# A gated linear attention over 128-token chunks by levels, rewritten over 64-token chunks with logarithms, angles and one masked score product

## The chip, the cores and the metric

The kernel runs on one core of one Trainium2 chip. A core has a matrix engine (PE, with its weight loads shown apart as PEld), a vector engine (DVE), an activation engine (ACT), a general engine (POOL), and SyncE (SP), whose queue issues most of the transfers. Each engine runs its own list of instructions in order; semaphores tie the lists together. The metric is device time in microseconds, less being better.

## The reference

Two blocks follow one another. The first is a recurrence with a complex decay for each feature, the second an MLP with ELU between its two products.

```python
B, H, S, D = (4, 8, 768, 48)
mag = np.sqrt(a_re * a_re + a_im * a_im)
scale = np.minimum(mag, 0.999) / (mag + 1e-06)
a_re_n, a_im_n = (a_re * scale, a_im * scale)
for t in range(S):
    ar, ai = (a_re_n[:, :, t, :, None], a_im_n[:, :, t, :, None])
    new_re = ar * S_re - ai * S_im
    new_im = ar * S_im + ai * S_re
    kv = np.einsum('bhd,bhe->bhde', k[:, :, t], v[:, :, t])
    S_re, S_im = (new_re + kv, new_im)
    y[:, :, t] = np.einsum('bhd,bhde->bhe', q[:, :, t], S_re)
# x = y as (B*S, H*D) = (3072, 384)
h = x @ w_in                       # (384, 2048)
g = np.where(h > 0.0, h, np.exp(np.minimum(h, 0.0)) - 1.0)
return g @ w_out                   # (2048, 384)
```

q, k and v are normal numbers times 0.1. a_re lies between 0.85 and 0.95, a_im is normal with a spread of 0.1. The two MLP weights arrive as float64 and are made float32 on the chip.

## The kernel before

A group is 256 tokens of one batch, two chunks of 128; there are twelve. Heads stand two by two on the partitions, tokens along the free dimension. Within a chunk, a query and a key meet at one of seven levels (blocks of 2, 4, .. 128 tokens). At each level `totals` (before the levels) multiplies decays over blocks, `scores` (the matmuls of L277) multiplies keys with queries, and `widen` carries both to blocks of twice the length by complex products: of queries on DVE, of keys on POOL (both in `product`, L247 to L251), with ACT copying the other half (L332). After every second level `values` masks the scores on DVE (L288) and multiplies them with values (L304). No logarithm and no division by a decay occurs. `normalise` makes the decays with a square root (L190) and a reciprocal (L192). `finish` adds what earlier chunks give (L343), transposes keys (L354) and makes the next state (L360). `begin` transposes inputs (L206).

`seam` moves y by ten transfers (L384) so that heads stand one after another. `hidden` (L397 and the activations L403 to L406) and `project` (L414, L419) are the MLP. They are called one level at a time in the next group's loop, so that they fall between its scores. `load_weights` (L154 to L176) takes one tile of float64 words through four DVE operations, an addition on POOL (L172) and a last DVE operation; four such tiles are called after each level of the first group until all 28 (12 of w_in, 16 of w_out) are done. The order of instructions on each engine is made by the tile framework's scheduler from the written order.

## Time and profile before

| | |
|---|---|
| median of 3 runs | 1701.83 us (1701.32 to 1703.79) |
| span of the profiled execution | 1704.6 us |
| the profiled execution's own time | not given apart from its span, which is 0.16% above the median |
| PE busy / weight loads | 1193.1 us (70%) / 922.5 us (54%) |
| DVE busy | 1289.6 us (76%) |
| POOL busy | 893.2 us (52%) |
| ACT busy | 439.2 us (26%) |
| bytes over the DMA queues | 69.67 MB, mean 41 GB/s |
| mean granted PE clock | 0.819 |

Busy time is the union of an engine's instructions. A matmul of float32 appears as two records in the profile, a transpose as one. A row of the timeline gives start, length, engine, line, operation, output and inputs, shapes, count, and in brackets the idle time before it with what ended it. A row of the groups gives the count, the busy time, the mean length in ns, and the idle time before with its releasers. A row of the waits gives the total, the number and the longest. A row of windows gives the stretch, busy time and count of PE, PEld, DVE, ACT and POOL, and then the granted clock, DMA share and rate.

### The profile page before, as it was taken

How to read it: one execution, taken by the hardware profiler on the slowest of the kernel's cores; microseconds unless marked ns; L12 is line 12 of the kernel's file. 1: busy time of each engine (PE TensorE's matmuls, PEld its weight loads, DVE VectorE, ACT ScalarE, POOL GpSimd, SP SyncE). 2: the span in 40 equal slices, each digit the busy share in tenths (PEclk: the TensorE clock that was granted, in tenths of full speed). 3: DMA queues.
4: the chain of work that ended last, by engine and by line, in shares of the span. 5: the costliest groups of instructions: out<-in, count | busy, mean ns of one | idle time of the engine just before them, and what ended most of it. 6: DMA issues, size and time to landing. Idle time of an engine off the chain costs nothing.

```text
span 1704.6 us, 26958 instructions
## 1 busy us (share of the span) xinstructions
PE 1193.1 (70%) x10464; PEld 922.5 (54%) x10464; DVE 1289.6 (76%) x1860; ACT 439.2 (26%) x865; POOL 893.2 (52%) x835
## 2 busy tenths in 40 slices
PE   3522368948848847866876874894893893894989
PEld 2521355637637636655654653663662763773766
DVE  7897888788788777867868868858858858858831
ACT  2010043124124123122322331331421521311313
POOL 6574464665465464544654654645545645635610
PEclk8555679778978978987996996996895996996999
DMA  5413330030031040022022013013012012010000
GB/s 108 107 54 108 116 60 11 18 72 17 18 67 26 18 76 16 15 59 37 12 51 49 12 47 51 8 38 65 8 38 54 20 34 45 13 33 23 2 19 10
DMA packets 156895, 69.67 MB, mean 41 GB/s; under 512 B 134496, under 2 KB 142432, under 8 KB 156768
## 3 DMA queue, kind: packets, MB, share of 16 engines
q1 hardware_dynamic: 156768, 67.94, 17.8%
q8 instruction: 84, 1.38, 0.4%
q14 instruction: 43, 0.35, 0.1%
HBM read 36.44 MB, written 4.72 MB: 24 GB/s over the span
## 4 chain that ended last, share of the span: by engine, by line
PE 45%; DVE 44%; issue 4%; POOL 3%; ACT 2%; DMA 1%; SPq 1%; POOLq 0%; DVEq 0%
PE bank L414 15%; PE a L277 11%; DVE pq L248 8%; DVE pq L247 8%; PE bank L397 8%; PE y L304 6%; DVE T L250 4%; DVE T L251 4%; DVE Q L251 3%; DVE Q L250 3%; DVE r L192 3%; DVE a_sb L288 2%; DVE g L406 2%; POOL wp L172 2%; DVE Q L224 2%
## 5 line engine op out<-in xcount | busy, mean ns | idle before, releaser
L277 PE MATMUL a<-Q,K 48*64 48x128 f32 (+1 forms) x4992 | 350.6, 291 | 334.7 <-DVE Q L250 291.3
L277 PEld LDWEIGHTS a<-Q,K 48*64 48x64 f32 x4992 | 307.1, 149 | 387.5 <-issue 275.9
L250 POOL TENSOR_TENSOR K<-pk,pk 128x256 f32<-128x256 f32 x168 | 145.0, 863 | 408.0 <-PE a L277 400.4
L397 PE MATMUL bank<-x,w_in 128*128 128x256 f32 x1152 | 305.3, 421 | 13.2 <-ACT er L404 8.9
L332 ACT COPY K<-K 128x256 f32<-128x256 f32 x336 | 137.5, 445 | 566.6 <-PE a L277 492.1
L397 PEld LDWEIGHTS bank<-x,w_in 128*128 128x128 f32 x1152 | 232.9, 209 | 66.1 <-issue 22.8
L414 PE MATMUL bank<-w_out,g 128*128 128x384 f32 x768 | 267.0, 501 | 0.1
L247 POOL TENSOR_TENSOR pk<-K,T 128x512 f32<-128x512 f32 x168 | 208.6, 1242 | 67.8 <-DVE T L250 50.4
L248 POOL TENSOR_TENSOR pk<-K,T 128x512 f32<-128x512 f32 x168 | 231.0, 1375 | 0.0
L250 DVE TENSOR_TENSOR Q<-pq,pq 128x256 f32<-128x256 f32 x168 | 109.5, 652 | 131.7 <-PE a L277 126.0
L414 PEld LDWEIGHTS bank<-w_out,g 128*128 128x128 f32 x768 | 143.7, 193 | 98.9 <-issue 11.2
L304 PE MATMUL y<-a_sb,vl 128*64 128x128 f32 (+1 forms) x1344 | 119.5, 316 | 98.3 <-DVE a_sb L288 98.3
L248 DVE TENSOR_TENSOR pq<-Q,T 128x512 f32<-128x512 f32 x168 | 174.7, 1040 | 0.0
L247 DVE TENSOR_TENSOR pq<-Q,T 128x512 f32<-128x512 f32 x168 | 166.6, 992 | 3.9
L304 PEld LDWEIGHTS y<-a_sb,vl 128*64 128x64 f32 (+1 forms) x1344 | 94.3, 163 | 134.3 <-DVE a_sb L288 115.5
L406 DVE SCALAR_TENSOR_TENSOR g<-ee,er 128x512 f32<-128x512 f32 x96 | 85.5, 893 | 89.8 <-ACT ee L405 89.8
L251 POOL TENSOR_TENSOR K<-pk,pk 128x256 f32<-128x256 f32 x168 | 149.0, 887 | 0.0
L251 DVE TENSOR_TENSOR Q<-pq,pq 128x256 f32<-128x256 f32 x168 | 131.8, 785 | 0.0
L288 DVE TENSOR_TENSOR a_sb<-a,masks 128x1024 f32<-128x1024 f32 x72 | 87.4, 1214 | 55.7 <-PE a L277 55.7
L403 ACT ACTIVATE ee<-bank 128x512 f32<-128x512 f32 x96 | 57.1, 595 | 234.0 <-PE bank L397 179.6
L247 DVE TENSOR_TENSOR pq<-T 128x512 f32<-128x512 f32 (+6 forms) x168 | 100.5, 598 | 17.5 <-ACT T L219 12.4
L248 DVE TENSOR_TENSOR pq<-T 128x512 f32<-128x512 f32 (+6 forms) x168 | 97.3, 579 | 0.0
(68 smaller groups left out, 1261.2 us busy)
## 6 DMA issues: line engine op xcount, KB each, us to landing
w<-in_moe_w_in_dram SPq DMA_DIRECT2D x12, 512.0 KB
vl<-vn SPq DMA_DIRECT2D x48, 128.0 KB
vl<-vn SPq DMA_DIRECT2D x96, 64.0 KB
vl<-vn SPq DMA_DIRECT2D x192, 32.0 KB
w<-in_moe_w_out_dram SPq DMA_DIRECT2D x16, 384.0 KB
ar<-in_a_re_dram SPq DMA_DIRECT2D x24, 192.0 KB
ai<-in_a_im_dram SPq DMA_DIRECT2D x24, 192.0 KB
kn<-in_k_dram SPq DMA_DIRECT2D x24, 192.0 KB
```

The lines of the kernel that those rows point to most:

```text
L247: eng.tensor_tensor(out=t1, in0=x, in1=y_re, op=ALU.mult)
L248: eng.tensor_tensor(out=t2, in0=x, in1=y_im, op=ALU.mult)
L250: eng.tensor_tensor(out=to_re, in0=seen(t1[:, 0]), in1=seen(t2[:, 1]), op=minus)
L251: eng.tensor_tensor(out=to_im, in0=seen(t1[:, 1]), in1=seen(t2[:, 0]), op=plus)
L277: nc.tensor.matmul(x["a"][ts(row, HP), z, ts(p, n)], lhsT=x["K"][rows, i, ts(p, C // 2)], rhs=x["Q"][rows, i, ds((p + 1) * C - n, n)], sta ...
L288: nc.vector.tensor_tensor(out=a, in0=x["a"].rearrange("p j (x t) -> p j x t", t=C), in1=masks[:, n].unsqueeze(1).unsqueeze(1).to_broadcast ...
L304: nc.tensor.matmul(to, **got, start=False, stop=False, skip_group_check=True)
L332: nc.scalar.copy(out=to[:, i, 1], in_=seen(old[:, i, 1]))
L397: nc.tensor.matmul(t[:, e], lhsT=w_in[:, i, ts(f0 + f + e, C)], rhs=x[:, i], start=(i == 0), stop=(i == NI - 1),)
L403: nc.scalar.activation(out=e, in_=t, func=AF.Relu, scale=-1.0)
L406: nc.vector.scalar_tensor_tensor(out=g[:, f : f + 2], in0=e, scalar=-1.0, in1=r, op0=ALU.add, op1=ALU.add)
L414: nc.tensor.matmul(t, lhsT=gs[f // FB][:, f % FB, ts(c, C)], rhs=w_out[:, f], start=(f == 0), stop=(f == NF - 1),)
```

## The change

The kernel is now split in two. The old one without its weights becomes `_general`, and stands behind a branch at the end (L906). Ahead of it stands a new one that does the whole computation. It takes units of 128 tokens of two batches (again 256 tokens, twelve units). `squares` and `logarithms` make, for each element, half the logarithm of the squared magnitude, capped, and the tangent's argument of the angle; `angles` takes the arctangent; `turns` and `decays` sum angles over the tokens and logarithms over 64 tokens by a matmul with a triangle of ones (L628, L650); `waves` takes sine and cosine, and `gated` multiplies keys by the inverse decay and queries by the decay, with sine and cosine beside each other (96 numbers a head). Then one score product for each 64 tokens (L712), masked once on DVE, replaces the seven levels; `states` (L733) and `values` (L757, L766) follow, and `hidden` (L801) and `project` (L817) as before, where ELU is now max(exp(min(h,0)) - 1, h), with one Relu less.

While it computes, it records for each unit the least a_re and the greatest |a_im|. `verdict` compares both with 0.7, and every engine reads the result and branches: where any element falls outside, the old kernel runs too and overwrites the output.

The order is written out by hand, in 15 steps of 16 slots: at step s the first stage (A) works on unit s, B on s - 1, C on s - 2, and the MLP (M) on s - 3. The weights are converted one a slot from step 0.

```diff
@@ -14,25 +14,31 @@
-C = 128  # tokens of a chunk, the length over which decays are multiplied out
+C = 128
+L = 64
...
+LEAST_RE = 0.7
+MAGIC = 1.5 * 2.0**23
+TURN = 6.2831850
...
-def tile_gateloop__then__act_elu_kernel(
+def _general(
...
+@with_exitstack
+def tile_gateloop__then__act_elu_kernel(
...
+    NB = 2
+    NU = B // NB * (S // C)
+    GT = NB * C
...
+    def work(shape):
+        return ps.tile(shape, FP32, tag="w", bufs=3, name="w")
...
+    def squares(u):
+        x = nat[u]
+        ar, ai = x["ar"], x["ai"]
+        nc.vector.tensor_reduce(
+            out=least[:, u : u + 1], in_=flat(ar), axis=mybir.AxisListType.X, op=ALU.min
+        )
+        nc.vector.tensor_reduce(
+            out=most[:, u : u + 1], in_=flat(ai), axis=mybir.AxisListType.X, op=ALU.max,
+            apply_absolute_value=True,
+        )
...
+    def logarithms(u):
+        x = nat[u]
+        ar, ai = x["ar"], x["ai"]
+        lm, lr = x["m2"], new("lr")
+        nc.scalar.activation(out=lm, in_=lm, func=AF.Ln)
+        nc.scalar.activation(out=lr, in_=ar, func=AF.Ln)
+        e, x0 = new("e"), new("x0")
+        nc.scalar.activation(out=x0, in_=lr, func=AF.Exp, scale=-1.0)
+        nc.scalar.activation(out=e, in_=lm, func=AF.Exp, scale=-0.5, bias=ln_eps)
+        nc.gpsimd.tensor_tensor(out=lr, in0=ar, in1=x0, op=ALU.mult)
+        nc.gpsimd.tensor_tensor(out=x0, in0=ai, in1=x0, op=ALU.mult)
+        x["l"] = new("l")
+        nc.vector.scalar_tensor_tensor(
+            out=flat(x["l"]), in0=flat(lm), scalar=2 * float(np.log(CAP)), in1=flat(e),
+            op0=ALU.min, op1=ALU.subtract,
+        )
+        nc.vector.scalar_tensor_tensor(
+            out=flat(x0), in0=flat(lr), scalar=-2.0, in1=flat(x0), op0=ALU.add, op1=ALU.mult
+        )
+        x["t"] = x0
...
+    def turns(u):
+        x = nat[u]
+        x["z"] = new("z")
+        for n in range(NB):
+            t = work([C, HD])
+            nc.tensor.matmul(
+                t, lhsT=sum_turns, rhs=x["th"][:, n].rearrange("p h d -> p (h d)"),
+                start=True, stop=True,
+            )
...
+    def decays(u):
+        x = nat[u]
+        x["E"], x["F"] = new("E"), new("F")
+        x["T"] = new("T", 3, [2 * D, NB, C // L, H])
+        for n in range(NB):
+            t = work([C, HD])
+            nc.tensor.matmul(
+                t, lhsT=sum_logs, rhs=x["l"][:, n].rearrange("p h d -> p (h d)"),
+                start=True, stop=True,
+            )
+            for key, sign in (("E", 1.0), ("F", -1.0)):
+                nc.scalar.activation(
+                    out=x[key][:, n].rearrange("p h d -> p (h d)"), in_=t, func=AF.Exp,
+                    scale=sign,
+                )
+        ends = dram.tile([NB, C // L, H, D], FP32, tag="ends", bufs=2, name="ends")
+        nc.sync.dma_start(
+            out=ends.rearrange("n c h d -> c n (h d)"),
+            in_=x["E"][L - 1 :: L].rearrange("p n h d -> p n (h d)"),
+        )
+        for i in range(2):
+            for n in range(NB):
+                nc.sync.dma_start(
+                    out=x["T"][ts(i, D), n].rearrange("p c h -> p (c h)"),
+                    in_=ends[n].rearrange("c h d -> d (c h)"),
+                )
...
+    def waves(u):
+        x = nat[u]
+        x["cs"] = new("cs", 1, [C, NB * H, 2, D])
+        z = x["z"].rearrange("p n h d -> p (n h) d")
+        nc.scalar.activation(out=x["cs"][:, :, 1], in_=z, func=AF.Sin, scale=TURN)
+        nc.scalar.activation(out=z, in_=z, func=AF.Abs)
+        nc.scalar.activation(
+            out=x["cs"][:, :, 0], in_=z, func=AF.Sin, scale=-TURN, bias=quarter
+        )
+    def gated(u):
+        x = nat[u]
+        shape = [C, NB * H, 2, D]
+        for key, by in (("k", "F"), ("q", "E")):
+            g = x[by]
+            nc.gpsimd.tensor_tensor(out=g, in0=x[key], in1=g, op=ALU.mult)
+            o = new(key + "g", 1 + (key == "k"), shape)
+            eng = nc.gpsimd if key == "k" else nc.vector
+            eng.tensor_tensor(
+                out=o, in0=g.rearrange("p n h d -> p (n h) d").unsqueeze(2).to_broadcast(shape),
+                in1=x["cs"], op=ALU.mult,
+            )
+            x[key + "g"] = o.rearrange("p (n h) i d -> p n h (i d)", n=NB)
...
+    def transposed(u, key, n):
+        x = nat[u]
+        x[key + "t", n] = o = new(key + "t", 2, [2 * D, H, C])
+        for h0 in range(0, H, 4):
+            t = work([2 * D, 4, C])
+            for h in range(4):
+                nc.tensor.transpose(t[:, h], x[key + "g"][:, n, h0 + h], ident)
+            nc.scalar.copy(out=o[:, h0 : h0 + 4], in_=t)
+    def scores(u, n):
+        x = nat[u]
+        t = work([C, H, L])
+        for h in range(H):
+            for c in range(C // L):
+                nc.tensor.matmul(
+                    t[ts(c, L), h], lhsT=x["kt", n][:, h, ts(c, L)],
+                    rhs=x["qt", n][:, h, ts(c, L)], start=True, stop=True,
+                )
+        x["a", n] = new("a", 2, [C, H, L])
+        nc.vector.tensor_tensor(
+            out=x["a", n], in0=t, in1=mask.unsqueeze(1).to_broadcast([C, H, L]), op=ALU.mult
+        )
+    def states(u, n):
+        x = nat[u]
+        b, s = where(u)
+        x["S", n] = [state.get(b + n)]
+        if s == S - C:
+            last = C // L - 1
+        else:
+            last = C // L
+        for c in range(last):
+            g = work([2 * D, H, D])
+            for h in range(H):
+                nc.tensor.matmul(
+                    g[:, h], lhsT=x["kg"][ts(c, L), n, h], rhs=vn[u % 2][ts(c, L), n, h, 0:D],
+                    start=True, stop=True,
+                )
+            old = x["S", n][-1]
+            new_s = new(f"S{n}", 5, [2 * D, H, D])
+            wide = x["T"][:, n, c].unsqueeze(2).to_broadcast([2 * D, H, D])
+            if old is None:
+                nc.vector.tensor_tensor(out=new_s, in0=g, in1=wide, op=ALU.mult)
+            else:
+                nc.vector.tensor_tensor(out=new_s, in0=g, in1=old, op=ALU.add)
+                nc.gpsimd.tensor_tensor(out=new_s, in0=new_s, in1=wide, op=ALU.mult)
+            x["S", n].append(new_s)
+        state[b + n] = x["S", n][-1]
+    def values(u, n):
+        x = nat[u]
+        y = ps.tile([C, C // L, 512], FP32, tag="y", bufs=1, name="y")
+        for p in range(NP):
+            for c in range(C // L):
+                at = x["S", n][c]
+                for j in range(2):
+                    h = 2 * p + j
+                    to = y[ts(j, HP), c, ts(p, L)]
+                    nc.tensor.matmul(
+                        to, lhsT=vn[u % 2][ts(c, L), n, h], rhs=x["a", n][ts(c, L), h],
+                        start=True, stop=at is None, skip_group_check=True,
+                    )
+            for c in range(C // L):
+                at = x["S", n][c]
+                for j in range(2):
+                    h = 2 * p + j
+                    if at is not None:
+                        nc.tensor.matmul(
+                            y[ds(j * HP, D), c, ts(p, L)], lhsT=at[:, h],
+                            rhs=x["qt", n][:, h, ts(c, L)], start=False, stop=True,
+                            skip_group_check=True,
+                        )
...
+    def hidden(u, f):
+        x = nat[u]
+        if f % 4 == 0:
+            x["g", f // 4] = new("g", 5, [C, 4, GT])
+        t = ps.tile([C, 2, GT], FP32, tag="mlp", bufs=3, name="mlp")
+        for e in range(2):
+            for i in range(NI):
+                nc.tensor.matmul(
+                    t[:, e], lhsT=w_in[:, i, ts(f + e, C)], rhs=x["x"][:, i],
+                    start=(i == 0), stop=(i == NI - 1),
+                )
+        e = new("ee", 4, [C, 2, GT])
+        nc.scalar.activation(out=e, in_=t, func=AF.Relu, scale=-1.0)
+        nc.scalar.activation(out=e, in_=e, func=AF.Exp, scale=-1.0)
+        nc.vector.scalar_tensor_tensor(
+            out=x["g", f // 4][:, f % 4 : f % 4 + 2], in0=e, scalar=-1.0, in1=t, op0=ALU.add, op1=ALU.max
+        )
+    def project(u, n, f0, f1):
+        x = nat[u]
+        if f0 == 0:
+            x["o"] = ps.tile([C, DM], FP32, tag="mlp", bufs=3, name="mlp")
+        for f in range(f0, f1):
+            nc.tensor.matmul(
+                x["o"], lhsT=x["g", f // 4][:, f % 4, ts(n, C)], rhs=w_out[:, f],
+                start=(f == 0), stop=(f == NF - 1),
+            )
...
+    def verdict():
+        fit, ones = cst.tile([C, NU], FP32, name="fit"), value(1.0, "ones")
+        nc.vector.tensor_scalar(
+            out=fit, in0=least, scalar1=LEAST_RE, scalar2=None, op0=ALU.is_ge
+        )
+        nc.vector.scalar_tensor_tensor(
+            out=fit, in0=most, scalar=LEAST_RE, in1=fit, op0=ALU.is_le, op1=ALU.mult
+        )
...
+        n = cst.tile([1, 1], FP32, name="n")
+        nc.vector.tensor_reduce(out=n, in_=t, axis=mybir.AxisListType.X, op=ALU.add)
+        nc.vector.tensor_scalar(
+            out=needs, in0=n, scalar1=C * NU - 0.5, scalar2=None, op0=ALU.is_lt
+        )
...
+    SLOTS = 16
+    A = [(1, squares), (4, logarithms), (9, angles), (10, carried)]
+    BB = [(2, turns), (4, decays), (9, waves), (10, gated)]
+    CC = []
+    for n in range(NB):
+        for at, fn in (
+            (0, lambda u, n=n: transposed(u, "q", n)), (1, lambda u, n=n: transposed(u, "k", n)),
+            (3, lambda u, n=n: scores(u, n)), (4, lambda u, n=n: states(u, n)),
+            (6, lambda u, n=n: values(u, n)),
+        ):
+            CC.append((at + 6 * n, fn))
+    CC.append((13, seam))
+    M = [lambda u, f=f: hidden(u, f) for f in range(0, NF, 2)]
+    M += [
+        lambda u, n=n, f=f: project(u, n, f, f + 4) for n in range(NB) for f in range(0, NF, 4)
+    ]
+    ctx.enter_context(tc.manual_schedule())
+    for step in range(NU + 3):
+        for s in range(SLOTS):
+            for late, stage in ((2, CC), (1, BB), (0, A)):
+                u = step - late
+                if 0 <= u < NU:
+                    for at, fn in stage:
+                        if at == s:
+                            fn(u)
+            if s == 5 and step + 1 < NU:
+                load_a(step + 1)
+            if s == 11 and 0 < step < NU:
+                load_qk(step)
+            if s == 14 and 0 < step < NU:
+                load_v(step)
+            if step < 3:
+                for w in weights[:1]:
+                    load_weights(*w)
+                weights = weights[1:]
+            u = step - 3
+            if u >= 0:
+                M[s](u)
+        if step == NU + 1:
+            verdict()
+    ctx.close()
+    with tc.If(nc.values_load(needs[0:1, 0:1]) > 0):
+        _general(tc, q, k, v, a_re, a_im, w_in, w_out, out)
```

Three places show what this does to the order. First DVE while weights are made, before (names as in the diff; w is a tile of float64 words, wp and wf its parts):

```order
L158 TENSOR_SCALAR wp<-w_406 128x512 [waits DMAHW1_49]
L158 TENSOR_SCALAR wp<-w_417 128x512 [waits DMAHW2_49]
L162 SCALAR_TENSOR_TENSOR wf<-w_406,wp 128x512 [waits DVE_49]
L162 SCALAR_TENSOR_TENSOR wf<-w_417,wp 128x512 [waits DVE_49]
L165 TENSOR_SCALAR wp<-wf 128x512 [waits DVE_49]
L173 TENSOR_SCALAR w_406<-w_406 128x512
L169 SCALAR_TENSOR_TENSOR wp<-w_406,wp 128x512 [waits DVE_49]
L165 TENSOR_SCALAR wp<-wf 128x512
L173 TENSOR_SCALAR w_417<-w_417 128x512
L176 SCALAR_TENSOR_TENSOR w_in<-w_406,wp 128x512 [waits Pool_49]
```

and now:

```order
L539 TENSOR_SCALAR wp<-w_124 128x512 [waits DMAHW7_49]
L543 SCALAR_TENSOR_TENSOR wf<-w_124,wp 128x512 [waits DVE_49]
L546 TENSOR_SCALAR wp<-wf 128x512 [waits DVE_49]
L550 SCALAR_TENSOR_TENSOR wp<-w_124,wp 128x512 [waits DVE_49]
L554 TENSOR_SCALAR w_124<-w_124 128x512
L557 SCALAR_TENSOR_TENSOR w_in<-w_124,wp 128x512 [waits DVE_49,Pool_49]
L539 TENSOR_SCALAR wp<-w_135 128x512 [waits DMAHW0_49]
```

A tile now ends, with its wait for POOL, before the next begins. Second, PE in the midst of the run, before (a: scores, bank: PSUM of the MLP and transposes):

```order
L277 MATMUL a<-Q,K 64x128 x32
L397 MATMUL bank<-x,w_in 128x256 x9
L304 MATMUL y<-a_sb,vl_80 64x128 x8
L397 MATMUL bank<-x,w_in 128x256 x3
L304 MATMUL y<-a_sb,vl_81 64x128 x8
```

and the first seven slots of a full step now:

```order
L704 MATMUL w<-ident,qg 96x128 x8
L801 MATMUL mlp<-x,w_in 128x256 x6
L704 MATMUL w<-ident,kg 96x128 x8
L801 MATMUL mlp<-x,w_in 128x256 x6
L628 MATMUL w<-th,sum_turns 128x384 x2
L801 MATMUL mlp<-x,w_in 128x256 x6
L712 MATMUL w<-qt,kt 64x64 x16
L801 MATMUL mlp<-x,w_in 128x256 x6
L733 MATMUL w<-vn_73,kg 96x48 x16
L650 MATMUL w<-l,sum_logs 128x384 x2
L801 MATMUL mlp<-x,w_in 128x256 x12
```

Each small piece of attention is now followed by a piece of the MLP of an older unit. Third, SP's queue around the seam (x: the MLP's input), before, where the loads of the next chunk's keys and queries follow it:

```order
L384 DMA x<-ysb 16x256
L384 DMA x<-ysb 32x256
L384 DMA x<-ysb 48x256 x2
L124 DMA kn_70<-in_k_dram 128x8x48
L124 DMA qn_66<-in_q_dram 128x8x48
L124 DMA kn_71<-in_k_dram 128x8x48
L124 DMA qn_67<-in_q_dram 128x8x48
```

and now:

```order
L509 DMA ai<-in_a_im_dram 128x8x48 x2
L509 DMA q<-in_q_dram 128x8x48 x2
L509 DMA k<-in_k_dram 128x8x48 x2
L825 DMA out_dram<-o 128x384
L787 DMA x<-y 48x256 x2
L787 DMA x<-y 32x256
L787 DMA x<-y 16x256
```

The loads of queries and keys, and with them their wait for POOL, have moved ahead of the seam.

244 lines of the change are left out of this document (186 added, 58 removed).

## The prediction

> **What bounds the kernel now.** I read the page from the top: the span, the busy line, the clock row, then the chain that ended last by engine and by line.
>
> ```profile
> span 1704.6 us, 26958 instructions
> PE 1193.1 (70%) x10464; PEld 922.5 (54%) x10464; DVE 1289.6 (76%) x1860; ACT 439.2 (26%) x865; POOL 893.2 (52%) x835
> ...
> PEclk8555679778978978987996996996895996996999
> ...
> PE 45%; DVE 44%; issue 4%; POOL 3%; ACT 2%; DMA 1%; SPq 1%; POOLq 0%; DVEq 0%
> PE bank L414 15%; PE a L277 11%; DVE pq L248 8%; DVE pq L247 8%; PE bank L397 8%; PE y L304 6%; DVE T L250 4%; DVE T L251 4%; DVE Q L251 3%; DVE Q L250 3%; DVE r L192 3%; DVE a_sb L288 2%; DVE g L406 2%; POOL wp L172 2%; DVE Q L224 2%
> ```
>
> No engine is full: PE and DVE hold the chain in turn, since a level's scores (L277) need queries that DVE has widened (L247 to L251), seven times in a row. The view of waits and two steps of the chain, one group of 256 tokens apart, say what that costs:
>
> ```profile
> PE a L277 <- DVE Q L250: 291.3, 19, 25.3
> ```
> ```profile
> 703.85 10.52 PE bank L414 x32
> ...
> 838.02 10.52 PE bank L414 x32
> ```
>
> A group takes 134.2 us, and twelve of them 1610 us of the span. So what matters is what one step of 256 tokens costs after the change, and what stands before the first full step. The sum below is one of spans; 1704.6 us stands 0.16% above the median of the runs shown, 1701.83, which I neglect.
>
> **MLP work that stays.** The timeline of the last group shows it alone, and a window shows the clock once PE is dense:
>
> ```profile
> 1658.51 22.12 PE L397 MATMUL bank<-x,w_in 128*128 128x256 f32 x92 [0.36 <-DMA x<-ysb]
> ...
> 1672.89 0.60 ACT L403 ACTIVATE ee<-bank 128x512 f32<-128x512 f32 x1 [0.99 <-PE bank L397]
> 1675.48 0.60 ACT L403 ACTIVATE ee<-bank 128x512 f32<-128x512 f32 x1 [0.99 <-PE bank L397]
> ...
> 1680.46 20.80 PE L414 MATMUL bank<-w_out,g 128*128 128x384 f32 x64
> ```
> ```profile
> 1600.00:1640.00 40.00, 37.01 (x276) 25.70 (x275) 28.18 (x31) 7.06 (x17) 22.36 (x21) 1.00 0.02 6
> ```
>
> A hidden call of 12 matmul records takes 2.59 us (1675.48 less 1672.89), a unit's eight 20.7; the projection's 64 take 20.8, or 0.325 each. Together 41.5 us a unit, before and after; the granted clock was 1.00 where PE was 93% busy with scores and MLP mixed.
>
> **Attention on PE, after.** The levels' scores and values go. A unit gets 32 transposes, 8 sums of 128x384 (turns, decays) and four kinds of small product: scores, states, values from scores, values from states, 64 records each. The nearest rows:
>
> ```profile
> 1641.46 1.61 PE L277 MATMUL a<-Q,K 48*64 48x64 f32 x44
> ...
> 1647.11 1.09 PE L354 MATMUL bank<-ident,K 128*128 128x128 f32 x8
> ...
> 1648.44 1.16 PE L360 MATMUL bank<-vn,kt 128*64 128x48 f32 x32 [0.24 <-ACT kt L355]
> ```
> ```profile
> 20.61 1.11 PE L206 MATMUL bank<-ident,ani 128*128 128x128 f32 x4 [0.29 <-POOL ani L198]
> ```
>
> Transposes: 1.09/8 = 0.136, so 4.4 us. Sums: 8 x 0.325 = 2.6. Scores and both kinds of values alternate between two column halves, as L360 does (1.16/32 = 0.036) and, by head, L277 (0.037): 3 x 64 x 0.037 = 7.1. The states (L733) use one and the same set of rows and columns eight times running, which no small row of before does. Between 0.036 (2.3 us) and a transpose's 0.136 with its 128-column load (8.7 us), I take 0.072, as if two of L360's halves no longer ran side by side: 4.6. Sum 18.7, bounds 16.4 to 22.8, so PE needs 60.2 us a step.
>
> The Trainium skill, "TensorE: Matmul & The Clock Gate", Part 3, The mechanism, says that a weight load overlaps running matmuls only when the row group differs; that speaks against the states, all of whose products of a half share their rows. The projection, whose loads and matmuls all span 128 rows, does not bear it out: 0.325 us each, dense, with a load for each. By the rule the states lie at the upper end of their bounds (8.7 us a step instead of 4.6).
>
> **Does anything else exceed 60 us a step?** Means by form, and an undisturbed POOL product:
>
> ```profile
> L185 ACT ACTIVATE m<-ar 128x768 f32<-128x768 f32 x12 | 10.1, 843 | 18.2 <-DMA ar<-in_a_re_dram 18.2
> L405 ACT ACT_TABLE_LOAD x10 | 12.8, 1283 | 0.2
> L403 ACT ACTIVATE ee<-bank 128x512 f32<-128x512 f32 x96 | 57.1, 595 | 234.0 <-PE bank L397 179.6 <-DVE g L406 53.0
> L406 DVE SCALAR_TENSOR_TENSOR g<-ee,er 128x512 f32<-128x512 f32 x96 | 85.5, 893 | 89.8 <-ACT ee L405 89.8
> L224 DVE TENSOR_TENSOR Q<-bank,T 128x1024 f32<-128x1024 f32 x24 | 29.1, 1211 | 2.2 <-PE bank L206 2.1
> ```
> ```profile
> 612.44 1.00 POOL L198 TENSOR_TENSOR ani<-ai,r 128x384 f32<-128x384 f32 x1
> ```
>
> ACT: ten passes over 768 (8.4 us), 26 over 512 from hidden, transposes and y (15.5), six of 384 (2.9), four table loads (5.1): 32 us. DVE: eight hidden results (7.1), a 1536-wide product at 1211/1024 per element (1.8), four passes over 768 (3.6), masks, sums, rounding (6): 19. POOL: five products over 768 (10), one over 1536 (4), four state products (4): 18. These lie under PE's 60.2, as do the removed Relu, the dropped square root and reciprocal, the test's two reductions and the branch's comparison: changing them moves nothing. If the cover went, the busiest, ACT, would still stay below PE.
>
> **Hand order: the waits.** Engines run as written, so I walked one step, 0 at its first transposes. At slot 4 ACT has the decays' four exponentials (2 us) and, for the next unit, two table loads and four logarithm passes (2.6 + 3.4) ahead of hidden 4's Relu, and behind it stand hidden 5 to 7 and the y and q copies. Hidden 7 wants hidden 4's bank of the three; DVE gives it back at about 30.3, PE arrives at 30.7. The second place is x for the next step:
>
> ```profile
> 896.99 0.51 SPq L124 DMA_DIRECT2D kn<-in_k_dram  x1
> ...
> 899.08 0.75 SPq L124 DMA_DIRECT2D qn<-in_q_dram  x1
> ```
> ```profile
> 1652.29 0.58 ACT L347 COPY ysb<-y 128x512 f32<-128x512 f32 x1 [3.41 <-PE y L343]
> 1652.90 6.22 SPq L384 DMA_DIRECT2D x<-ysb  x10
> 1656.10 2.04 PE L397 MATMUL bank<-x,w_in 128*128 128x256 f32 x4 [3.86 <-DMA x<-ysb]
> ...
> 1701.30 0.48 ACT L419 COPY o<-bank 128x384 f32<-128x384 f32 x1 [9.84 <-PE bank L414]
> ```
>
> In SP's queue the ten seam DMAs now stand behind the four q and k loads, which wait for POOL's gating (768 + 1536 + 768 wide: 7.5 us), itself behind the second states at about 43: 50.5, plus 2.9 for four issues, plus 5.6 until the last x lands (1652.90 to 1658.51): 59.4. The next hidden is due at 61.5. Both places just hold; I add 1.8 us for half-microsecond waits on work tiles. A full step is 62 us.
>
> **Before the first full step.** Steps 0 and 1 turn 28 weight tiles into float32. Before, their DVE rows interleave two tiles; now DVE sits at each tile's last operation (L557) until POOL has added. Rows for one tile of each size, and the first tile's arrival:
>
> ```profile
> 17.04 1.27 DVE L158 TENSOR_SCALAR wp<-w 128x512 uint32<-128x512 uint32 x1
> ...
> 121.57 0.42 DVE L173 TENSOR_SCALAR w<-w 128x512 uint32<-128x512 uint32 x1
> 121.90 0.68 DVE L169 SCALAR_TENSOR_TENSOR wp<-w,wp 128x512 f32<-128x512 uint32 x1
> ...
> 124.25 0.68 DVE L176 SCALAR_TENSOR_TENSOR w_in<-w,wp 128x512 f32<-128x512 uint32 x1
> ...
> 161.85 0.35 DVE L173 TENSOR_SCALAR w<-w 128x384 uint32<-128x384 uint32 x1
> 162.12 0.55 DVE L169 SCALAR_TENSOR_TENSOR wp<-w,wp 128x384 f32<-128x384 uint32 x1
> ...
> 164.15 0.56 DVE L176 SCALAR_TENSOR_TENSOR w_out<-w,wp 128x384 f32<-128x384 uint32 x1 [0.88 <-POOL wp L172]
> ```
> ```profile
> 122.73 1.31 POOL L172 TENSOR_TENSOR wp<-wp,wf 128x512 f32<-128x512 f32 x1 [2.57 <-DVE wp L169]
> ...
> 162.81 1.31 POOL L172 TENSOR_TENSOR wp<-wp,wf 128x384 f32<-128x384 f32 x1 [1.87 <-DVE wp L169]
> ```
>
> A w_in tile: two short and two long operations, 2.2, gaps 0.2, handover to POOL 0.15, 1.31, back 0.2, 0.68: 4.8 us. A w_out tile: 4.0. Together 12 x 4.8 + 16 x 4.0 = 122 us on one path. With the start at 17, DVE's work for two units (11.5) and its wait for POOL's first gating (7), DVE is through at 157, the first q product being out 8 us earlier. Step 2 has PE cold (four transposes took 1.11 us at the start, eight 1.09 late) and no MLP to hide behind: transposes, mask and states to about 165; then ACT's exponentials and logarithms to 171 ahead of the second half's copies; scores and states to 178; gating to 186; q and k issues, seam: first hidden at 194. Low 180, if the weights overlap more; high 235, if they run as contended as the row at 17.04 (1.27 for 0.42).
>
> **Sum.** 194 + 11 x 62 + a last step of MLP alone, 41.5, + 6 behind it = 924 us. Of the 6, 3.3 are before's own end (1701.30 to 1704.6); the register read and branch no row shows: between 0 and 5, half is taken.
>
> **Rivals.**
> 1. Loads of the states show in full (their upper bound): 64 x 0.136 instead of 0.072 adds 4.1 us to 11 steps, 969 us. For it, the one form no row shows; against it, the dense projection.
> 2. The relay slips. The two places of the walk have margins of 0.4 and 2 us. A hidden result on DVE takes 0.68 undisturbed, and 0.893 in the mean quoted above:
>
> ```profile
> 696.67 0.68 DVE L406 SCALAR_TENSOR_TENSOR g<-ee,er 128x512 f32<-128x512 f32 x1
> ```
>
> At means instead of undisturbed rows, with POOL half slower beside DVE, hidden 4's bank is some 4 us late, x some 5: 9 us a step, 1023 us. For it, the narrow margins and that no wait is hidden by a scheduler; against it, DVE and POOL are a third full.
> 3. Slower: the branch is taken. One element with a_re under 0.7 or |a_im| over 0.7 runs the old levels after everything, at twelve groups of 134.2: 924 + 1610 = 2534 us. The inputs (0.85 to 0.95; a spread of 0.1, so seven spreads) speak against it; so would a test that counts wrongly.
>
> **Chances.** Forecast's case (880 to 960) 0.60, rival 1 0.12, rival 2 0.25, rival 3 0.01, and 0.02 for faster still; none ends near 1702. From the bounds: 180 + 11 x 58 + 45 = 863 at the low end, 235 + 11 x 72 + 47 = 1074 at the high. I give 880 to 1035, which takes in rival 1 and about half of what rival 2 spreads over. Faster by over 0.2% (what a measurement here can tell) 0.99, within it 0, slower 0.01.
>
> **What would show it.** Right: steps of about 62 us from 194 on, PE over 95% busy at a clock of 1.00, weights taking 122 us with DVE waiting on POOL at L557, first hidden matmul near 194. Wrong: idle PE before L801 put down to DVE's L808 or to x's DMA (rival 2); L733 above 0.1 us a record (rival 1); level code in the trace (rival 3).

## The result and the profile after

The changed kernel takes **924.21 us** (median of 4 runs, 923.49 to 924.97); the one before took 1701.8 beside it. The ratio is 0.5427, with a 95% interval of 0.542 to 0.5435. 924 us was predicted. The profiled execution has a span of 923.1 us.

Five rows of the page of the kernel after: busy time, PE's slices, its clock, and the chain that ended last by engine:

```profile
PE 748.3 (81%) x5346; PEld 553.3 (60%) x5346; DVE 302.4 (33%) x454; ACT 369.1 (40%) x555; POOL 226.8 (25%) x159
...
PE   0110002849999999999999999999999999999997
...
PEclk9999999559999999999999999999999999999999
...
PE 56%; POOL 13%; issue 11%; DVE 8%; SPq 8%; DMA 4%; POOLq 0%; ACT 0%; DVEq 0%
```

DVE's work fell from 1289.6 to 302.4 us, PE's from 1193.1 to 748.3. PE is all but idle for seven of the forty slices (some 160 us) and full from the tenth on; the clock row shows 9 throughout that part. So the two engines no longer alternate, and PE sets the pace of the steps. The chain names POOL, DVE and SP too, for two reasons. One is what stands ahead of the first step. The other is the way of x, the MLP's input, between steps, as three pieces of the chain (start, length, what) show:

```profile
563.38 1.77 POOL E L686
...
574.75 1.96 DMA x<-y
576.85 1.96 PE mlp L801 x8
```

POOL's gating ends at 565.15. Then SP issues the loads of q and k, an output store and the ten transfers of the seam, the last of these lands at 576.71, and only then PE can go on with the hidden product.

Three windows of the kernel after (columns: stretch, its length, busy us and instructions of PE, PEld, DVE, ACT, POOL; granted clock, DMA share, GB/s): a steady one, the one that ends with the last weight tile, and the one from there to the first hidden product:

```profile
500.00:560.00 60.00, 59.34 (x444) 44.51 (x439) 17.84 (x24) 29.82 (x46) 14.89 (x12) 1.00 0.25 48
```
```profile
17.00:159.80 142.80, 11.55 (x60) 6.97 (x60) 102.43 (x181) 26.85 (x32) 52.76 (x39) 1.00 0.35 98
159.80:201.00 41.20, 25.74 (x221) 20.55 (x221) 12.57 (x16) 16.34 (x23) 13.36 (x8) 0.54 0.28 44
```

In the steady window PE is busy for 98.9%, and ACT, DVE and POOL use half of it or less. In the start, PE does 11.55 us of work in 142.8 while DVE turns the tiles and does the first stages of two units, and DVE is busy for 102.4 of them, not all.

PE's timeline over one step, from the first values of a unit's second half to the same place a unit later:

```profile
499.48 0.34 PE L757 MATMUL y<-a,vn 64*64 64x64 f32 x8
...
516.81 1.04 PE L704 MATMUL w<-ident,kg 128*96 128x128 f32 x8
517.68 2.75 PE L801 MATMUL mlp<-x,w_in 128*128 128x256 f32 x12
520.27 1.45 PE L628 MATMUL w<-th,sum_turns 128*128 128x384 f32 x4
...
525.33 2.86 PE L801 MATMUL mlp<-x,w_in 128*128 128x256 f32 x12
528.12 2.62 PE L733 MATMUL w<-vn,kg 64*96 64x48 f32 x32
530.66 1.56 PE L650 MATMUL w<-l,sum_logs 128*128 128x384 f32 x4
532.06 5.34 PE L801 MATMUL mlp<-x,w_in 128*128 128x256 f32 x24
...
561.46 0.34 PE L757 MATMUL y<-a,vn 64*64 64x64 f32 x8
```

This step is 61.98 us (561.46 less 499.48), the longest of eight like ones: their first hidden products stand 61.53 to 61.98 us apart, 61.65 in the mean (493.2 us from 267.0 to 760.3). A record's own length overlaps the next one's, so costs are read from start to start: eight transposes 0.87 us (517.68 less 516.81), 32 records of the states 2.54 us (530.66 less 528.12), a hidden call 2.59 to 2.79, four sums of logarithms 1.40. What PE waited for at the hidden products, over the whole run, stands in their group:

```profile
L801 PE MATMUL mlp<-x,w_in 128*128 128x256 f32 x1152 | 269.2, 385 | 7.7 <-DMA x<-y 6.4 <-issue 0.9 <-DVE g L808 0.4
```

Of the 6.4 us for x, 4.4 stand at the first hidden call of all (2.99, 0.44 and 0.96), where the first x arrives piece by piece.

The start, on DVE and PE, up to the first hidden product:

```profile
27.78 0.69 DVE L557 SCALAR_TENSOR_TENSOR w_in<-w,wp 128x512 f32<-128x512 uint32 x1 [1.15 <-POOL wp L553]
...
139.73 2.14 DVE L557 SCALAR_TENSOR_TENSOR w_out<-w,wp 128x384 f32<-128x384 uint32 x1 [0.90 <-POOL wp L553]
146.94 1.76 DVE L689 TENSOR_TENSOR qg<-E,cs 128x1536 f32<-128x1536 f32 x1 [5.07 <-POOL E L686]
...
177.03 1.84 DVE L597 SCALAR_TENSOR_TENSOR l<-m,e 128x768 f32<-128x768 f32 x1 [9.08 <-ACT e L593]
...
194.18 1.76 DVE L689 TENSOR_TENSOR qg<-E,cs 128x1536 f32<-128x1536 f32 x1 [7.96 <-POOL E L686]
```
```profile
200.99 1.19 PE L801 MATMUL mlp<-x,w_in 128*128 128x256 f32 x2 [2.99 <-DMA x<-y]
```

DVE waits for POOL in every tile (1.15 us here), then for the gating (5.07), for ACT's logarithms (9.08) and for the next gating (7.96). The first hidden product starts at 201.

### The profile page after: what moved, and what is told of

The parts are those of the page before. It is cut to its first block, busy times and chain, and to the rows that moved or that the text cites. A ratio compares the mean times of both kernels' runs of the same rounds, so it can differ in the third digit from the quotient of the medians.

```text
span 923.1 us, 13005 instructions
## 1 busy us (share of the span) xinstructions
PE 748.3 (81%) x5346; PEld 553.3 (60%) x5346; DVE 302.4 (33%) x454; ACT 369.1 (40%) x555; POOL 226.8 (25%) x159
## 4 chain that ended last, share of the span: by engine, by line
PE 56%; POOL 13%; issue 11%; DVE 8%; SPq 8%; DMA 4%; POOLq 0%; ACT 0%; DVEq 0%
PE mlp L801 25%; PE mlp L817 15%; PE w L733 4%; SPq L787 4%; POOL kg L689 3%; PE w L704 3%; SPq L509 3%; POOL wp L553 3%; PE w L712 2%; PE y L766 2%; DVE wf L543 2%; POOL F L686 2%; POOL E L686 2%; DVE wp L550 2%; PE y L757 2%
## 5 line engine op out<-in xcount | busy, mean ns | idle before, releaser
L801 PE MATMUL mlp<-x,w_in 128*128 128x256 f32 x1152 | 269.2, 385 | 7.7 <-DMA x<-y 6.4
L817 PE MATMUL mlp<-w_out,g 128*128 128x384 f32 x768 | 258.5, 490 | 0.0
L801 PEld LDWEIGHTS mlp<-x,w_in 128*128 128x128 f32 x1152 | 214.9, 191 | 46.1 <-issue 6.3
L817 PEld LDWEIGHTS mlp<-w_out,g 128*128 128x128 f32 x768 | 143.2, 190 | 92.7
L808 DVE SCALAR_TENSOR_TENSOR g<-ee,mlp 128x512 f32<-128x512 f32 x96 | 64.9, 685 | 264.3 <-ACT ee L807 264.2
L806 ACT ACTIVATE ee<-mlp 128x512 f32<-128x512 f32 x96 | 56.9, 592 | 124.0 <-PE mlp L801 124.0
L823 ACT COPY o<-mlp 128x384 f32<-128x384 f32 x24 | 11.5, 479 | 223.3 <-PE mlp L817 223.3
L733 PEld LDWEIGHTS w<-vn,kg 64*96 64x96 f32 x704 | 59.8, 172 | 18.1 <-issue 9.6
L733 PE MATMUL w<-vn,kg 64*96 64x48 f32 x704 | 62.8, 257 | 8.2 <-DVE z L636 8.2
L807 ACT ACTIVATE ee<-ee 128x512 f32<-128x512 f32 x96 | 60.5, 630 | 2.8
L628 PE MATMUL w<-th,sum_turns 128*128 128x384 f32 x48 | 18.9, 520 | 43.2 <-DMA ai<-in_a_im_dram 43.2
L689 POOL TENSOR_TENSOR kg<-F,cs 128x1536 f32<-128x1536 f32 x12 | 41.5, 3458 | 0.9
L766 PE MATMUL y<-qt,S 96*48 96x64 f32 x704 | 40.6, 233 | 0.0
```

The costliest lines, as they stand in the source:

```text
L689: eng.tensor_tensor(out=o, in0=g.rearrange("p n h d -> p (n h) d").unsqueeze(2).to_broadcast(shape), in1=x["cs"], op=ALU.mult,)
L733: nc.tensor.matmul(g[:, h], lhsT=x["kg"][ts(c, L), n, h], rhs=vn[u % 2][ts(c, L), n, h, 0:D], start=True, stop=True,)
L766: nc.tensor.matmul(y[ds(j * HP, D), c, ts(p, L)], lhsT=at[:, h], rhs=x["qt", n][:, h, ts(c, L)], start=False, stop=True, skip_group_check= ...
L801: nc.tensor.matmul(t[:, e], lhsT=w_in[:, i, ts(f + e, C)], rhs=x["x"][:, i], start=(i == 0), stop=(i == NI - 1),)
L806: nc.scalar.activation(out=e, in_=t, func=AF.Relu, scale=-1.0)
L807: nc.scalar.activation(out=e, in_=e, func=AF.Exp, scale=-1.0)
```

## The experiments

Times are medians against the same kernel before; "first hidden" is the start of the first hidden product on PE (L801; L803 or L794 where the edit moves the lines), "step" the distance of two like rows near 500 us, with the mean of the eight like steps in parentheses where they differ.

| kernel | time, us | ratio to before, 95% | first hidden, us | step, us |
|---|---|---|---|---|
| the change | 924.21 | 0.5427 (0.542 to 0.5435) | 201.0 | 61.98 (61.65) |
| second Relu | 922.24 | 0.5415 (0.5403 to 0.5426) | | |
| states alternated | 915.31 | 0.5379 (0.5364 to 0.5393) | 197.8 | 60.78 (60.94) |
| q and k loads later | 909.68 | 0.5342 (0.5332 to 0.5351) | 193.5 | 61.08 |
| both of these | 891.81 | 0.5230 (0.5222 to 0.5239) | 193.2 | 59.32 |
| both, tiles spread | 889.93 | 0.5221 (0.5213 to 0.523) | 176.6 | |
| tiles in pairs | 920.43 | 0.5408 (0.5396 to 0.5419) | 194.8 | |
| addition on DVE | 907.66 | 0.5326 (0.5318 to 0.5334) | 183.2 | |
| no test | 916.21 | 0.5377 (0.5369 to 0.5386) | 194.0 | |
| scheduler's order | 860.14 | 0.5047 (0.5039 to 0.5056) | 140.2 | 60.93 |
| that, states alternated | 851.45 | 0.4994 (0.4986 to 0.5001) | 140.1 | 59.89 |
| that, sums one slot later | **842.70** | 0.4952 (0.4943 to 0.4961) | 140.0 | 58.81 |
| branch taken | 2514.9 (one run) | | | |

### What a step costs on PE: the states

```diff
-        for c in range(last):
-            g = work([2 * D, H, D])
-            for h in range(H):
+        gs = [work([2 * D, H, D]) for c in range(last)]
+        for h in range(H):
+            for c in range(last):
                 nc.tensor.matmul(
-                    g[:, h], lhsT=x["kg"][ts(c, L), n, h], ...
+                    gs[c][:, h], lhsT=x["kg"][ts(c, L), n, h], ...
```

> Edit: the states of both 64-token halves (rows 0 to 63 and 64 to 127 of the array) are issued in turn instead of one half after the other; nothing else. Theory (PE's own work paces a full step): the record falls from 0.080 us to about 0.037, that is 64 x 0.043 = 2.75 us a step, and all of it comes back: 924 - 11 x 2.75 = 894 us. Rival A (loading 96 columns binds whatever the rows): 0.080 stays, 924. Rival B (the relay of ACT and DVE holds the step): the record falls, the step stays at 61.3 us, 924.

Measured: 915.31 us, between the two. PE's timeline of this run (L733 is the states; lines after L745 stand two higher), and the group of L803 from its page:

```profile
520.48 1.56 PE L733 MATMUL w<-vn,kg 64*96 64x48 f32 x32
521.97 0.91 PE L650 MATMUL w<-l,sum_logs 128*128 128x384 f32 x2
```
```profile
L803 PE MATMUL mlp<-x,w_in 128*128 128x256 f32 x1152 | 269.2, 385 | 17.1 <-DMA x<-y 16.8 <-DVE g L810 0.2
```

32 records now take 1.49 us (521.97 less 520.48) instead of 2.54: 0.047 each instead of 0.079, 2.1 us a step. But in the mean the step became only 0.7 us shorter (61.65 to 60.94; 1.2 near 500 us): PE came to the seam earlier, x did not, and the wait for it grew from 6.4 to 16.8 us over the run. Of the 1.4 us that are missing, some 0.9 went to x and 0.46 to the sums behind the states, as a later run shows. The Trainium skill, "TensorE: Matmul & The Clock Gate", Part 3, The mechanism, lets a weight load overlap only a matmul on another row group: alternating the two groups of rows saves 0.032 us a record, which goes that way; the 0.136 that the rival of the prediction took was not reached. The edit also makes the products alternate between two PSUM tiles, and no run keeps the two apart, so that the rows are the cause is argued and not shown.

### What a step waits for: x

```diff
-            if s == 11 and 0 < step < NU:
+            if s == 13 and 0 < step < NU:
                 load_qk(step)
```

> Edit: the loads of q and k move from slot 11 to slot 13, behind the seam's ten transfers in SP's queue. Theory (x comes late because SP stands at the q load until POOL has gated): the waits of hidden for x (6.4 us put down to it, and 0.7 of issue in each step) go and the first hidden starts 5 us earlier: 912 to 917 us. Rival (q and k then arrive late and gating waits): 924 or more.

Measured: 909.68 us, a little better than the theory. With SP's ten seam transfers ahead of the loads, the steady windows have no wait left:

```profile
500.00:560.00 60.00, 60.00 (x452) 44.87 (x450) 17.83 (x24) 29.85 (x46) 16.87 (x11) 1.00 0.26 44
```

Every full step is now 61.08, and that is work: before, each had lost 0.45 to 0.90 us to the seam, 0.57 in the mean. Of the 16.0 us between the two spans (923.1 and 907.1) 7.5 come from the start, where the first x stood behind the same loads, and 3.6 from the first step behind it (66.0 to 62.4). Both edits together:

> Both edits that were run alone: the states of the two 64-row halves alternate, and SP's q and k loads stand behind its ten seam transfers. Theory: the alternated states take 2 us less of PE a step, and alone they gave back half of it because the next step's x came through SP too late, behind the q and k loads that wait for POOL's gating; with the loads out of the way the whole gain stays. 909.7 (loads moved alone) less 2.0 x 11 to 12 steps = 886 to 888, and PE's wait for x in the steady steps under 0.3 us a step. Rival: a shorter PE step makes x late whatever stands before the seam on SP (the values or the mask on DVE are what the transfer waits for): then half of the gain is lost again as in the run of the halves alone, 909.7 - 9 = 900 or more, and PE's wait for x is near 1 us a step.

Measured: 891.81 us. 17.9 of the 22 to 24 us stay, so the theory holds in kind. What is missing is on PE's timeline of this run:

```profile
506.28 0.91 PE L650 MATMUL w<-l,sum_logs 128*128 128x384 f32 x2
507.39 0.91 PE L650 MATMUL w<-l,sum_logs 128*128 128x384 f32 x2 [0.20 <-DVE S L745]
508.14 5.34 PE L803 MATMUL mlp<-x,w_in 128*128 128x256 f32 x24
```

The alternated states hold two PSUM banks of the three at once, and the second pair of sums waits for DVE to read one out; with the break in the run of four, the sums take 1.86 us (508.14 less 506.28) instead of 1.40. That is 0.46 us a step, some 5 us in all.

### Is ACT covered?

```diff
+        r = new("ee", 4, [C, 2, GT])
         nc.scalar.activation(out=e, in_=t, func=AF.Relu, scale=-1.0)
+        nc.scalar.activation(out=r, in_=t, func=AF.Relu)
         nc.scalar.activation(out=e, in_=e, func=AF.Exp, scale=-1.0)
...
-            out=..., in0=e, scalar=-1.0, in1=t, op0=ALU.add, op1=ALU.max
+            out=..., in0=e, scalar=-1.0, in1=r, op0=ALU.add, op1=ALU.add
```

> Edit: ELU as in the kernel before, with a second Relu pass on ACT and a sum on DVE, so ACT gets 8 x 0.59 = 4.7 us more a step and each bank of the MLP is read for 0.6 us longer. Theory (PE paces, ACT is covered): 924 to 930 us, with at most half a microsecond of wait for a bank in a step. Rival (the relay has a margin of 0.4 us only and pays each further microsecond in full): 4 us a step more, 968.

Measured: 922.24 us. ACT's busy time rose from 369.1 to 406.0 us and the time did not rise at all. The relay of banks between PE, ACT and DVE has room for it.

### What a weight tile costs

The first edit puts the last operation of a tile (L557) behind the first five of the next, so that DVE has work while POOL adds; the second moves the addition to DVE.

```diff
-        nc.vector.scalar_tensor_tensor(
+        return lambda: nc.vector.scalar_tensor_tensor(
...
-                for w in weights[:1]:
-                    load_weights(*w)
+                end = load_weights(*weights[0]) if weights else None
+                if open_tile:
+                    open_tile.pop()()
+                if end:
+                    open_tile.append(end)
```

> Edit: the last DVE operation of a weight tile (L557) is issued after the first five of the next tile, so DVE does not wait for POOL. Theory (one path DVE - POOL - DVE sets the start): the 28 waits of 0.9 to 1.15 us go, 28.5 us in all, less some contention of the two engines: first hidden matmul at 172 to 180 instead of 201, 896 to 903 us. Rival (the tiles' arrival or their five buffers set the start): 924.

Measured: 920.43 us. The waits at L557 are gone, and L557 itself became as long as they had been. DVE and POOL of this run:

```profile
24.35 1.75 DVE L557 SCALAR_TENSOR_TENSOR w_in<-w,wp 128x512 f32<-128x512 uint32 x1
...
28.68 1.75 DVE L557 SCALAR_TENSOR_TENSOR w_in<-w,wp 128x512 f32<-128x512 uint32 x1
```
```profile
24.18 1.38 POOL L553 TENSOR_TENSOR wp<-wp,wf 128x512 f32<-128x512 f32 x1 [2.28 <-DVE wp L550]
```

POOL's addition ends at 25.56, and L557 ends at 26.10: 0.54 us later, about its own undisturbed length of 0.69. So DVE stood still until POOL was through, and the wait of 1.15 was only renamed: a w_in tile takes 4.33 us (28.68 less 24.35) instead of 4.43, and the first hidden product came at 194.8 where the theory had 172 to 180. The Trainium skill, "SBUF — State Buffer", SBUF: two separate sides, has a DVE operation with two inputs in SBUF and one of GpSimd lock each other out of a shared port for a whole instruction; these rows agree.

```diff
-        nc.gpsimd.tensor_tensor(out=p, in0=p, in1=f, op=ALU.add)
+        nc.vector.tensor_tensor(out=p, in0=p, in1=f, op=ALU.add)
```

> The one addition of each weight tile moves from POOL to DVE, in the hand-made order. Theory: what a tile pays for POOL is the hand-over, 1.15 us of waiting in a w_in tile and 0.88 in a w_out tile; an addition on DVE takes what DVE's other operations with two tensors take, 0.69 and 0.56, and none of DVE's operations runs beside POOL's then. 12 x 0.46 + 16 x 0.32 = 10.6 us earlier at most, also without the 2.14 us of the tiles that POOL stretches: 911 to 917, first hidden product near 190. Rival: DVE's addition costs as much as the wait (DVE was the serial engine in either case), 921 to 927.

Measured: 907.66 us, better than the theory's best. DVE and POOL of this run:

```profile
22.96 0.42 DVE L539 TENSOR_SCALAR wp<-w 128x512 uint32<-128x512 uint32 x1
...
27.00 0.42 DVE L539 TENSOR_SCALAR wp<-w 128x512 uint32<-128x512 uint32 x1
...
132.14 1.75 DVE L689 TENSOR_TENSOR qg<-E,cs 128x1536 f32<-128x1536 f32 x1
```
```profile
99.23 2.11 POOL L686 TENSOR_TENSOR F<-k,F 128x768 f32<-128x768 f32 x1
```

A w_in tile takes 4.04 us (27.00 less 22.96), 0.39 less. Besides, POOL no longer has the additions in its order, runs the first gating at 99 to 107 beside the tiles, and DVE's q product has no wait (5.07 before). The theory had priced the hand-over and not POOL's queue. The first hidden product comes 17.8 us earlier: 9 to 10 by the tiles, 5 by the gating, and the rest by DVE's waits for a tile to arrive, 3.9 us before and none here. Why tiles no longer arrive late was not traced. DVE is still held up beside POOL's products, as the last section shows.

### Where the start lies: the hand-made order

The tiles spread over three steps (5, 7 and 16 instead of 16, 12 and 0) and paired as above, with both edits of PE and SP:

```diff
-            if step < 3:
+            if ((step == 0 and s in (0, 2, 5, 7, 9)) or (step == 1 and s in (0, 3, 5, 6, 7, 8, 9))
+                or step == 2 or (step == 3 and open_tile)):
```

> The two edits of the other run, and the 28 weight tiles spread over three steps (5, 7 and 16 instead of 16, 12 and 0), the last operation of each behind the first five of the next. Theory: what delays the first hidden product is DVE's serial work, 122 us of tiles and the work of three steps with its waits for POOL and for ACT; tiles that stand beside the logarithms of the third step fill DVE's waits of 9 and 8 us there and its wait of 5 us for the gating in the second, so that the first hidden product comes 10 to 25 us earlier than the 193 of the other run, and the time is 887 - 10 to 25 = 862 to 877. Rival: tiles that are moved into the third step delay its squares, sums and masks in DVE's order by as much as they fill, as each waits behind a whole tile of 3.5 us: the first hidden product stays at 193 or comes later, 887 or more.

Measured: 889.93 us, 1.9 less than without. The first hidden product came 16.6 us earlier (176.6 for 193.2), as the theory had it, but the step that it opens became 13.9 us longer (74.3 for 60.4), so the theory fails on the time. PE's timeline shows the first hidden calls at once and then nothing, and ACT's shows why:

```profile
176.61 4.82 PE L803 MATMUL mlp<-x,w_in 128*128 128x256 f32 x12
...
196.05 1.65 PE L628 MATMUL w<-th,sum_turns 128*128 128x384 f32 x2 [10.52 <-ACT kt L705]
```
```profile
192.99 0.60 ACT L808 ACTIVATE ee<-mlp 128x512 f32<-128x512 f32 x1 [15.56 <-DVE w_out L557]
```

Six tiles stand in DVE's list from 175.5 to 196.7, ahead of the first hidden result. In the code, the parts of a tile share the four buffers of `ee`, the output of the first Relu. So ACT waits for a tile's last operation until 192.9, and the copy of the keys, for which PE waits, stands behind that Relu on ACT. A tile moved later in an order by hand delays what stands behind it, also on engines that never touch the tile. The order itself was the next suspect:

```diff
-    ctx.enter_context(tc.manual_schedule())
```

> The order by hand is given up: the same instructions, ordered by the scheduler's own rules (it takes the angles and logarithms of unit 0 ahead of the weights, and cuts the product of two hidden calls otherwise). Theory: the gain of this change is in what the engines no longer do, 1702 to 924, and only the margins of the hand-made order (0.4 us for a bank, 2 us for x) hang on the order: 5 to 10 us a step lost at most, 930 to 1030. Rival: the order carries much of the gain; engines that wait for each other in turn cost 20 us a step or more, 1150 or more.

Measured: **860.14 us, 64 less than the hand-made order**. Neither the theory nor the rival had a gain. The start of this run as a window, DVE's first q product and last tile, and where PE takes up the MLP:

```profile
17.00:149.40 132.40, 44.71 (x317) 33.66 (x318) 123.32 (x183) 58.35 (x68) 67.87 (x44) 0.61 0.55 129
```
```profile
62.36 2.82 DVE L689 TENSOR_TENSOR qg<-E,cs 128x1536 f32<-128x1536 f32 x1
...
158.14 0.56 DVE L557 SCALAR_TENSOR_TENSOR w_out<-w,wp 128x384 f32<-128x384 uint32 x1 [0.58 <-POOL wp L553]
```
```profile
140.19 1.91 PE L801 MATMUL mlp<-x,w_in 128*128 128x256 f32 x4
```

The outputs of the two orders, as the view of line L823 sums them up, of the hand-made order first:

```profile
L823 ACT COPY o<-mlp x24: 478/478/480, 253.7 to 916.8; 128x384 f32<-128x384 f32 x24
```
```profile
L823 ACT COPY o<-mlp x24: 462/479/480, 196.5 to 850.6; 128x384 f32<-128x384 f32 x24
```

The spans differ by 64.7 us: the first output comes 57.2 earlier, the way from the first output to the last is 9.0 shorter (654.1 against 663.1), and 1.5 is given back behind it. The scheduler cuts tiles apart, operation by operation, and lays the logarithms, masks and gating of the first units between them: the first q product stands at 62 instead of 147. The tiles are hardly through earlier, at 158.7 instead of 159.8. But the first hidden product, at 140, no longer waits for the last of them, nor for the chain of 41 us that stands behind the last tile in the hand-made order and in which DVE works for 12.6. DVE is busy for 93% of its start (123.3 of 132.4) instead of 72%, yet that is not all work: some 36 us of the 123.3 are operations that lasted longer than their shortest like record, nearly all of them beside an operation of POOL, against some 13 of the 102.4. A hand-made order with the w_out tiles beside the first hidden calls was not tried: a tile's words use the buffers of the hidden results.

With the states alternated as well:

> The scheduler's order and the states of the two halves alternated. Theory: in the scheduler's order PE has no wait between its steps (60.00 us busy of 60), so that every microsecond taken off PE's instructions comes off the time: 2.0 us a step for 10 to 12 of the 12 units, 860.1 - 20 to 24 = 836 to 840. Rival: as in the hand order, a shorter PE step meets the next limit (x through SP, or the gating on POOL, which the scheduler let run to 17.5 us in 60), and half the gain goes: 848 or more.

Measured: 851.45 us: the rival was nearer, half the gain is lost, but not to x. PE's timeline:

```profile
524.07 0.91 PE L650 MATMUL w<-l,sum_logs 128*128 128x384 f32 x2
525.80 0.91 PE L650 MATMUL w<-l,sum_logs 128*128 128x384 f32 x2 [0.82 <-DVE S L745]
```

It is the bank again, 0.82 us where it had been 0.20, since DVE's read of the states comes later in this order. The account closes: 2.1 gained, 0.82 waited and 0.24 for the cut run of sums (2.48 us with the wait, against 1.42) leave 1.04, and the step fell from 60.93 to 59.89. So the sums of logarithms were put one slot later, behind a hidden call:

```diff
-    BB = [(2, turns), (4, decays), (9, waves), (10, gated)]
+    BB = [(2, turns), (5, decays), (9, waves), (10, gated)]
```

> The scheduler's order with alternated states, and the sums of logarithms one place later, so that a call of the hidden product (2.6 us of PE) stands between the second states and them. Theory: what took half of the gain there is a PSUM bank: the alternated states hold two of the three banks at once, and the second pair of sums waits 0.82 us for DVE to read the states out (and runs 0.2 us longer cut in two); with the hidden call between them the bank is free, the step falls from 59.89 to 58.8-59.1, and the time from 851.5 to 841-844, with no wait of PE in the steady steps. Rival: PE's shorter step meets another limit at once (POOL's gating, x, the copies on ACT): 849 or more, and the wait shows on another line.

Measured: **842.70 us, as the theory said**; a step is 58.81 and PE has no wait in it:

```profile
500.00:560.00 60.00, 60.00 (x468) 44.70 (x466) 18.72 (x26) 38.55 (x55) 16.27 (x11) 1.00 0.28 47
```

This version beats both kernels: half of the time before, and 8.8% less than the change.

### What the test and the branch cost

```diff
-        nc.vector.tensor_reduce(out=least[:, u : u + 1], ...)
-        nc.vector.tensor_reduce(out=most[:, u : u + 1], ...)
...
-        if step == NU + 1:
-            verdict()
...
-    with tc.If(nc.values_load(needs[0:1, 0:1]) > 0):
-        _general(tc, q, k, v, a_re, a_im, w_in, w_out, out)
```

> The test is left out: no smallest modulus and largest angle, no verdict, no branch and no code behind it (so it would be wrong for other values). Theory: in the steady steps the two reductions of 0.94 us are covered on DVE; in the first three steps they stand in DVE's serial chain (1.72 us each, the third between the last tile at 159.7 and the first hidden product), and after the last store the branch has to read its verdict on every engine, an estimate of 1 to 3 us of the 5.9 behind the last copy. 924.2 - 4 to 8 = 916 to 920. Rival: all of it is covered but the end, 921 to 924.

Measured: 916.21 us (914.99 to 918.03), the theory's edge. The last copy of the hand-made order with the test, and without:

```profile
916.77 0.48 ACT L823 COPY o<-mlp 128x384 f32<-128x384 f32 x1 [9.84 <-PE mlp L817]
```
```profile
909.71 0.48 ACT L816 COPY o<-mlp 128x384 f32<-128x384 f32 x1 [9.84 <-PE mlp L810]
```

Behind the end of that copy the span runs on for 5.9 us with the branch (923.1 less 917.25) and 3.0 without (913.2 less 910.19): the branch costs 2.9. The first hidden product comes 7.0 us earlier; three pairs of reductions at 1.72 explain 5.2 of that, the other 1.8 were not traced. The steps gain nothing.

```diff
-LEAST_RE = 0.7
+LEAST_RE = 0.9
```

> The bound on the modulus in the test is raised from 0.7 to 0.9, so that the values of this input do not pass and the branch at the end is taken: everything is computed twice, the second time by the code by levels. Theory: the walk and its verdict, 923, then the code by levels at its own pace, 12 units of about 134 us as before the change, 2500 to 2560. Rival: the branch costs more than its body (code that has to be fetched, engines that drain), 2600 or more; or the second part finds its weights ready and is shorter by its start, 2400 to 2470.

Measured: 2514.9 us in one run, as the theory said. The second part starts after the walk and runs for 1590 us:

```profile
0.00:923.00 923.00, 746.67 (x5346) 552.03 (x5346) 302.37 (x454) 369.95 (x556) 229.53 (x172) 0.92 0.25 51
923.00:2513.00 1590.00, 1157.37 (x10464) 896.06 (x10464) 1207.72 (x1692) 436.81 (x863) 847.88 (x790) 0.85 0.18 36
```

The first window has 5346 records on PE, as many as the whole normal run, and the second has the 10464 of the old kernel. So in the normal run the branch is not taken.

## Why the prediction was right

The mechanism held in the main: PE paces full steps from the first hidden product on, and the start is DVE's serial work on tiles and then a chain through ACT, PE, POOL and SP. One step of the walk, the arrival of x, failed without showing in the time. And the time agrees to 0.2 us because errors of 7 to 8 us cancelled, which is luck:

| term | predicted, us | measured, us |
|---|---|---|
| tile of w_in, of w_out | 4.8, 4.0 | 4.43, 3.58 |
| DVE through with the tiles | 157 | 159.8 |
| first q product out | 149 | 148.7 |
| first hidden product | 194 | 201.0 |
| transposes, sums | 4.4, 2.6 | 3.6, 2.7 |
| states | 4.6 | 5.1 |
| scores and both values | 7.1 | 7.2 |
| MLP in a step | 41.5 | 42.4 |
| waits in a step | 1.8, for work tiles | 0.9, for x |
| full step | 62 | 61.98 near 500 us, 61.65 in the mean |
| last x landed, after the step's first transposes | 59.4 | 64.3 |
| mean of the eleven | 62 | 61.3 |
| behind the last copy | 6 | 5.9 |

**The start was mis-sized by 7 us**, in two places. Tiles by themselves took 11.6 us less than 122 (12 x 4.43 + 16 x 3.58 = 110.4), 5 of them since POOL's addition for a w_out tile takes 0.99 and not the 1.31 of the row that was used. But six tiles beside a product of POOL were stretched by 1.58 us each (2.14 and 2.27 for 0.56 and 0.69), DVE waited 3.9 us for tiles to arrive, and the last one ended 2.8 us late. Then the chain behind it, put at 37 us, took 41.2: the second product of q stood at 194.18, where the first hidden product had been expected, and the q and k loads and the seam came after it. That the loads stood in the seam's way, as the walk had said, cost 7.5 us there.

**The step was right as a sum of opposite errors.** In the step near 500 us transposes and waits were put too high (0.8 and 0.9), states and MLP too low (0.5 and 0.9): a hidden call among other products takes up to 2.79 us and not 2.59. The eleven steps are 674.1 us (875.1, where the last unit's MLP begins, less 201.0). The first takes 66.0, eight take 61.5 to 62.0, and the last two 59.3 and 55.6, since they have half of the states and the very last has no sums. So the start is 7.0 us too long and the steps are 7.9 us too short, and neither was predicted.

**The wait for x was misread.** The walk had the last x land at 59.4 (its own terms, 50.5, 2.9 and 5.6, add to 59.0), 2 us before it is due. Counted from the first transposes at 512.45, POOL's gating ended at 52.7. SP was through the four loads, and an output store that the walk had left out, at 56.4. The last x landed at 64.3. From the first issue to the last landing the ten transfers take 7.9 us (568.82 to 576.71) and not 5.6: the 1658.51 that the prediction read as the last landing is where PE goes on after the seventh, while the row of the ten issues runs to 1659.12. So there was no margin. PE itself came to the next hidden call at 62.85 and not at 61.5, and had two of the three parts of x to begin with, so that only 0.45 to 0.90 us were lost. The 1.8 us that the sum had for waits stood for work tiles instead, and in its full steps the kernel after shows no wait for one. That the 1.8 covered the loss to x is luck as well.

The register read and branch, for which no row stood, were put at 2.5 us; leaving them out saved 2.9.

**Of the rivals**, the full loads of the states (969) fall: 0.079 us a record against 0.136, though keeping to the same rows (and the same PSUM tile) does cost 0.032. The slipped relay (1023) falls too: PE waited 0.4 us in all for a hidden result, and 37 us more of ACT changed nothing. The half of it that held is x: its margin was already crossed, by 0.45 to 0.90 us a step, and some 0.9 of the 2.1 us that the alternated states took off PE were lost to it until SP's order changed. The branch is not taken.

**What the prediction did not ask** is what the order by hand is worth. It counted the waits of that order, in the steps and in the start, and took them for the price of the change; the same instructions in the scheduler's order need 64 us less, 57 of them ahead of the first output.
